# Order of the first loads in a fused attention and feed-forward kernel: a load ahead of the identity, beacon keys on another queue, up weights ahead of the masks

## The chip, the cores and the metric

The kernel runs on one core of a Trainium2 chip. The metric is device time in microseconds (us), the lower the better. A profiled execution has a span, from the first to the last instruction, and a time of its own, which is a little longer.

## The reference

Attention over 8 sequences of 8 heads, 576 tokens and 64 dimensions, with 16 "beacon" keys and values in front that every query sees; behind it a feed-forward layer without bias, with a leaky ReLU.

```python
k_all = np.concatenate([beacon_k, k], axis=2)
v_all = np.concatenate([beacon_v, v], axis=2)
scores = scale * np.matmul(q, k_all.transpose(0, 1, 3, 2))
causal[:, Nb:] = np.triu(np.ones((S, S), dtype=bool), k=1)
scores = np.where(causal, -1000000000.0, scores)
a = np.exp(scores - scores.max(-1, keepdims=True))
a /= a.sum(-1, keepdims=True) + 1e-09
x = np.matmul(a, v_all)          # then (batch, token, head*dim): 4608 x 512
h = x @ w_in                     # 512 x 2048
out = np.maximum(0.01 * h, h) @ w_out   # 2048 x 512
```

## The kernel before

The work is done by pairs of heads: pair `g` is heads 2h and 2h+1 of sequence `g // 4`, so there are 32 pairs, four to a sequence. Everything is in bf16 with sums in float32.

For a pair, `t_q` (L229, L235) turns queries and keys on TensorE (PE) with an identity matrix and copies them out of PSUM. `score` (L253, L262) makes the transposed scores in four parts on PE, and ScalarE (ACT) takes the exponential into `aT`. `mask` (L275) zeroes the upper triangles of `aT` on GpSimd (POOL), five selects for a pair. `value` (L342 to L352) multiplies by the values, with a column of ones that yields the sums, and VectorE (DVE) divides. `x_transposes` or `x_turn` put the result into `xT`. From then on `up` (L395, L402) makes one 128-wide block of the hidden layer for 512 tokens, and `down` (L433) a quarter of an output tile. PE alternates between these and the attention of later sequences; the last part is feed-forward alone. From pair 8 on queries and keys are loaded in natural order (`load_natural`, L157) and turned by DMA from SP (`turn_pair`, L165).

Each engine executes its instructions in the order in which the program text issues them. For the head, the first eight pairs, this order is written out by hand in strings of steps that `run` reads. `l3.0` loads pair 3's queries and `l3.1` its keys (L145), `V1.2` value block 2 of sequence 1 (L200), `s2.1` is part 1 of pair 2's scores, `m2.1` a part of its masks, `q3` and `k3` its transposes, `v0.0` the first half of pair 0's values, `x1` the transpose of its result, `u` and `d` an up and a down step, `i0` and `i1` the two halves of the up weights (L118), `o0` and `o1` of the down weights (L124), `N8.0` and `T8` pair 8's loads and turns. `w6` and `W0.0.4` are blank matmuls whose results nobody reads.

All loads that change the type from float32 to bf16 are issued by GpSimd, on one queue, between its masks. The beacon keys are loaded as float32 into `bk_raw` (L171): those of sequences 0 and 1 from ScalarE, those of sequences 2 to 7 in one load of 128 x 6 x 64 elements (192 KB) from SP. They are cast to bf16 into `bk`, the later ones by GpSimd (L174) after pair 6's masks; PE then turns them (L180) and they are copied to the key tiles of pairs 8 and on. The text has the load from SP after `s3.3`, but no earlier instruction stands in SP's list except the load of pair 0's keys `first_k` (L151), so SP issues it in the first microseconds.

In the built program GpSimd's loads take eight completion semaphores in turn, and a load waits on its semaphore for the load eight places ahead of it to land.

Of the kernel before, what the change touches and what calls it, by code (L numbers as in the profile page):

```python
# [15 lines left out]
def kernel(  # L16
# [11 lines left out]
    nc = tc.nc  # L28

    B, H, S, D = q.shape  # L30
# [112 lines left out]
    def load_qk(g, which):  # L143
        b, hp, grp, rows = where(g)
        loaded["qk", g, which] = nc.gpsimd.dma_start(  # L145
            out=raw_of(b, grp)[which][rows],
            in_=(q, k)[which][b, 2 * hp : 2 * hp + 2].rearrange("h (p i) d -> p h i d", i=RI),
        )
# [21 lines left out]
    def load_beacon_k(b0, b1, eng):  # L170
        eng.dma_start(out=bk_raw[:, b0:b1], in_=beacon_k[b0:b1].rearrange("b h n d -> (h n) b d"))  # L171
# [19 lines left out]
    def load_v_cast(b, c):  # L191
        dst = v_bufs[b % 2]
        lo = 0
        if c == 0:
            nc.gpsimd.dma_start(
                out=dst[0:NB, 0, :, 0:D], in_=beacon_v[b].rearrange("h p d -> p h d")
            )
            lo = NB
        n = ROWS[c] - lo
        nc.gpsimd.dma_start(  # L200
            out=dst[lo : ROWS[c], c, :, 0:D],
            in_=v[b, :, OFF[c] : OFF[c] + n].rearrange("h p d -> p h d"),
        )
# [9 lines left out]
    def beacon_columns(g, copy):  # L213
        b, hp = divmod(g, NPAIR)
        copy(out=k_bufs[g % NK][:, 0:NB], in_=bkT[:, b, hp])
# [26 lines left out]
    def score(g, n):  # L242
        qT, kT = qk[g]
        if n == 0:
            probs[g] = a_bufs[g % NA]
        aT = probs[g]
        parts = SCORES[n]
        sc = ps_sc.tile([128, 2, 512], FP32, name="sc", tag="sc")
        c0 = parts[0][3]
        for c, q0, w, col in parts:  # L250
            for par in range(2):
                ps_ = slice(par * 64, par * 64 + 64)
                nc.tensor.matmul(  # L253
                    out=sc[:, par, col - c0 : col - c0 + w],
                    lhsT=kT[ps_, c * 128 : (c + 1) * 128],
                    rhs=qT[ps_, q0 : q0 + w],
                    start=True,
                    stop=True,
                    skip_group_check=True,
                )  # L260
        w = sum(p[2] for p in parts)
        nc.scalar.activation(  # L262
            out=aT[:, :, c0 : c0 + w], in_=sc[:, :, 0:w], func=AF.Exp, scale=0.125
        )
# [3 lines left out]
    def mask(g, part):  # L268
        aT = probs[g]
        for lo, n, rows in MASKS[part]:  # L270
            triangle(aT, lo, n, rows)
# [231 lines left out]
    def finish(g, eng=0):  # L503
        if eng < 2 and g in xs:
            x_transposes(g, (dve, act)[eng])
        ready[0] = chunks_with(g)
        if g % NPAIR == NPAIR - 1:
            turn[0] = 1

    def run(steps):  # L510
        for step in steps.split():
            op, a = step[0], [int(x) for x in step[1:].split(".")] if step[1:] else []
            if op == "s":
                score(*a)
            elif op == "m":
                mask(*a)
            elif op == "v":
                value(*a)
            elif op == "x":
                finish(*a)  # L520
            elif op == "l":
                load_qk(*a)
            elif op == "V":
                load_v_cast(*a)
            elif op == "N":
                load_natural(*a)
            elif op == "T":
                turn_pair(a[0])
            elif op == "y":
                x_turn(a[0])  # L530
            elif op == "q" or op == "k":
                t_q(a[0], 0 if op == "q" else 1, (dve, act)[a[1] if len(a) > 1 else 0])
            elif op == "b":
                beacon_columns(a[0], (dve, act, pool)[a[1]])
            elif op == "u":
                up()
            elif op == "P":
                moe1_early(*a)
            elif op == "d":
                down()  # L540
            elif op == "w":
                unused(*a)
            elif op == "W":
                unused_ahead(*a)
            elif op == "i":
                load_w_in(a[0])
            elif op == "o":
                load_w_out(a[0])
            else:
                raise ValueError(step)  # L550
# [11 lines left out]
    with order:  # L562
        load_first_keys()
        load_beacon_k(0, 2, nc.scalar)
        nc.vector.memset(blank, 0.0)  # L565
        run("l0.0")
        make_identity(nc, ident)
        make_ones()
        run("l1.0 l1.1 l2.0 l2.1 V0.0 V0.1 V0.2 l3.0 l3.1 V0.3 V0.4 l4.0 l4.1")
        make_pads()  # L570
        unused(24)
        cast_beacon_k(0, 2, nc.scalar.copy)
        beacon_transposes(0, 2)
        unused(10)
        nc.scalar.copy(out=k_nat0[:, :, 0], in_=first_k[:, 0])
        nc.vector.tensor_copy(out=k_nat0[:, :, 1], in_=first_k[:, 1])
        run("q0.1 k0 w6 s0.0 m0.0 q1 s0.1 k1 w6 s0.2 m0.1 w6 s0.3 m0.2 i0")
        run("w6 s1.0 m1.0 q2 s1.1 k2 w6 s1.2 m1.1 w6 s1.3 m1.2 W0.0.4 s2.0 m2.0 W0.0.4 s2.1 q3 l5.0 l5.1 W0.0.4 s2.2 k3 v0.0 m2.1 s2.3 m2.2 i1 W0.1.4 s3.0 m3.0 v1.0 s3.1 v0.1 s3.2 v1.1 m3.1 l6.0 l6.1 s3.3 x0.1 m3.2")
        load_beacon_k(2, B, nc.sync)
        run("v2.0 l7.0 l7.1 q4 v2.1 V1.0 V1.1 x1 k4.1 v3.0 v3.1 x2.1 s4.0 s4.1 x3 m4.0 V1.2 V1.3 V1.4 u s4.2 u s4.3 m4.1 m4.2 o0 u q5 k5 u")  # L580
        run("s5.0 s5.1 m5.0 u u s5.2 s5.3 m5.1 m5.2 o1 u q6 k6 u v4.0 u v4.1 s6.0 s6.1 m6.0 u y4 N8.0 N8.1 u s6.2 s6.3 m6.1 m6.2 u")
        cast_beacon_k(2, B, nc.gpsimd.tensor_copy)
        run("q7 u k7 u v5.0 u v5.1 y5 N9.0 s7.0 s7.1 m7.0 d v6.0 v6.1 d y6 T8 s7.2 s7.3 m7.1 m7.2 N9.1 T9")
        beacon_transposes(2, B)
        run("b8.2 b9.2 b10.2 b11.2 u v7.0 v7.1 d d d d N10.0 N10.1 V2.0 V2.1 V2.2 V2.3 V2.4 d d N11.0 N11.1 x7")


        CUTS = [(0, 512, 1024, 1536, 1664), (0, 384, 896, 1376, 1664), (0, 224, 736, 1248, 1664)]
        BLOCKS = [((0, 0),), ((0, 1),)], [((0, 2),), ((0, 3), (1, 0))], [((1, 1),), ((1, 2),)], [((1, 3), (2, 0)), ((2, 1),)], [((2, 2),), ((2, 3),)]
        FIRST = 2 * NPAIR  # L590

        def block(g0, i):
            for tile in BLOCKS[i]:
                stretch([(g0 + r, CUTS[r][n], CUTS[r][n + 1]) for r, n in tile])

        events = []
        for g in range(FIRST, NG):
            if g > FIRST + 3:
                events.append((g - 3.6, 0, run, ("N%d.0" % g,)))
                events.append((g - 3.1, 0, run, ("N%d.1" % g,)))  # L600
            if g > FIRST + 1:
                events.append((g - 2.0, 0, run, ("T%d" % g,)))
            if g > FIRST + 3:
                events.append((g - 1.9, 0, run, ("b%d.2" % g,)))
            events.append((g + 2.25, 3, value, (g, 0)))
            events.append((g + 2.62, 4, value, (g, 1)))
            events.append((g + 2.63, 5, x_turn, (g,)))
            if (g - FIRST) % 3 == 0:
                for i in range(5):
                    events.append((g + (0.31 if g == FIRST else 0.01) + 0.6 * i, 2, block, (g, i)))  # L610
        ends = [FIRST]
        for g in range(FIRST, NG):
            events.append((g + 3.5, 2, finish, (g, 2)))
            if g % NPAIR == NPAIR - 1:
                ends.append(g + 3.5)
        for b in range(3, B):
            for n in range(NKB):
                events.append((4 * b - 0.9 + 0.3 * n, 6, load_v_cast, (b, n)))
        events.sort(key=lambda e: e[:2])
        KEPT = 3  # L620
        first_down[0] = 4
        w, d0 = 0, done1[0] + done2[0]
        for at, _, what, args in events:
            while w + 2 < len(ends) and at > ends[w + 1]:
                w, d0 = w + 1, done1[0] + done2[0]
            todo = 2 * NF * ready[0] - KEPT - d0
            aim = d0 + todo * (at - ends[w]) / (ends[w + 1] - ends[w])
            while done1[0] + done2[0] < aim and fill():
                pass
            what(*args)  # L630
        while done2[0] < NCH * NF:
            fill()
# [30 lines left out]
```

## Time and profile before

| What | Value |
|---|---|
| Median of 4 runs (lowest to highest) | 342.98 us (341.84 to 346.03) |
| Profiled execution: its own time, its span | 342.78 us, 341.1 us |
| Granted TensorE clock, mean | 0.997 |
| Busy: PE, ACT, POOL, DVE | 331.7, 186.8, 180.4, 81.8 us |
| First up matmul on PE | 25.26 us |
| Landing of the first load of queries | 5.47 us |
| Landing of the second half of the up weights | 31.15 us |

The profile lists busy time of each engine, the chain of waits that ended last, and groups of instructions by line of the program. In the timelines the columns are the start and the length in us, then engine, line, operation, the tile written and the tile read, and in brackets the idle time ahead and what ended it. A load has two times: the issue, for which the engine is busy, and the landing, given as a time after the start of the issue.

### The profile page before, as it was taken

The numbers are of one execution on the slowest core, as the hardware profiler recorded it, in microseconds if no ns is written. First come the engines' busy times: TensorE is split into PE (matmuls) and PEld (weight loads), VectorE is DVE, ScalarE is ACT, GpSimd is POOL, SyncE is SP. The second block draws the span as 40 slices with busy tenths as digits, with TensorE's granted clock in tenths as the row PEclk, the third lists the DMA queues.
The fourth block names the chain that finished last, engine by engine and source line by source line (L and its number), as shares of the span: only waits on it lengthen the run. The fifth ranks groups of instructions, "written<-read, shape, count | busy, mean of one in ns | idle before, by whom it ended". The sixth has DMA issues, their size and how long they took to land.

```text
span 341.1 us, 7423 instructions
## 1 busy us (share of the span) xinstructions
PE 331.7 (97%) x2982; PEld 167.7 (49%) x2982; DVE 81.8 (24%) x199; ACT 186.8 (55%) x280; POOL 180.4 (53%) x354
## 2 busy tenths in 40 slices
PE   8899899999998999999999999999999999999995
PEld 6573455445453545454454554544555544444442
DVE  4372344121232113221222122212321220000111
ACT  4978662669643864479257753775457205633300
POOL 8995768889997686398476854772211000000000
PEclk9999999999999999999999999999999999999998
DMA  8999999999999998999999999998220120000021
GB/s 156 149 211 174 129 185 153 184 156 165 167 145 177 168 134 109 152 124 144 122 146 120 118 151 122 158 122 79 81 82 17 32 97 33 0 31 33 31 92 62
DMA packets 155042, 40.16 MB, mean 118 GB/s; under 512 B 145152, under 2 KB 149376, under 8 KB 155008
## 3 DMA queue, kind: packets, MB, share of 16 engines
q0 software_dynamic: 100784, 18.34, 74.9%
q1 hardware_dynamic: 53808, 21.16, 33.0%
q8 instruction: 23, 0.38, 0.5%
q10 hardware_dynamic: 416, 0.20, 0.2%
q14 instruction: 11, 0.09, 0.1%
HBM read 37.22 MB, written 9.44 MB: 137 GB/s over the span
## 4 chain that ended last, share of the span: by engine, by line
PE 77%; DMA 13%; POOL 7%; SPq 1%; issue 1%; DVE 0%; ACT 0%; POOLq 0%
PE acc L395 33%; PE acc L433 30%; PE av L342 7%; PE sc L297 5%; DMA v_aug<-in_v_dram 4%; DMA w_in_sb<-in_moe_w_in_dram 4%; POOL aT L275 2%; DMA k_nat<-in_k_dram 2%; DMA xT<-x_nat 2%; POOL v_aug L200 2%; DMA q_raw<-in_q_dram 1%; PE sc L253 1%; POOL k_nat L157 1%; PE tp L229 1%; PE av L483 1%
## 5 line engine op out<-in xcount | busy, mean ns | idle before, releaser
L395 PE MATMUL acc<-xT,w_in_sb 128*128 128x512 bf16 x576 | 139.0, 379 | 1.4 <-DMA xT<-x_nat 1.4
L433 PE MATMUL acc<-w_out_sb,gT 128*128 128x512 bf16 x576 | 136.6, 379 | 0.0
L402 ACT ACTIVATE gT<-acc 128x512 bf16<-128x512 f32 x144 | 85.2, 606 | 80.0 <-PE acc L395 79.3
L310 ACT ACTIVATE aT<-sc 128x1024 bf16<-128x1024 f32 (+3 forms) x96 | 76.8, 866 | 47.4 <-PE sc L297 45.7
L275 POOL TENSOR_SCALAR_AFFINE_SELECT aT<-aT 128x256 bf16<-128x256 bf16 (+2 forms) x160 | 58.0, 396 | 67.6 <-ACT aT L310 61.0
L433 PEld LDWEIGHTS <-gT 128*128 128x128 bf16 x576 | 53.7, 98 | 62.3 <-issue 2.5
L395 PEld LDWEIGHTS <-w_in_sb 128*128 128x128 bf16 x576 | 52.2, 98 | 60.5 <-issue 2.7
L445 DVE COPY osb<-acc 128x512 f32<-128x512 f32 x35 | 24.2, 692 | 92.1 <-PE acc L433 91.4
L351 DVE RECIPROCAL rec<-av 128x6 f32<-128x6 f32 (+1 forms) x64 | 12.1, 188 | 135.5 <-PE av L342 135.5
L342 PEld LDWEIGHTS <-aT 128*128 128x128 bf16 (+1 forms) x960 | 36.3, 98 | 14.1 <-issue 4.2
L342 PE MATMUL av<-v_aug,aT 128*128 128x65 bf16 (+1 forms) x960 | 40.3, 194 | 0.9 <-POOL aT L275 0.7
L200 POOL DMA_DIRECT2D v_aug<-in_v_dram x40 | 34.1, 861 | 4.2 <-DMA w_in_sb<-in_moe_w_in_dram 4.0
L157 POOL DMA_DIRECT2D k_nat<-in_k_dram x48 | 34.8, 730 | 2.3 <-DMA v_aug<-in_v_dram 1.2
L157 POOL DMA_DIRECT2D q_nat<-in_q_dram x48 | 34.8, 729 | 2.3 <-DMA v_aug<-in_v_dram 1.4
L352 DVE TENSOR_TENSOR x_nat<-av,rec 128x384 bf16<-128x384 f32 (+1 forms) x64 | 31.4, 491 | 2.2
L262 ACT ACTIVATE aT<-sc 128x1024 bf16<-128x1024 f32 (+3 forms) x32 | 26.4, 877 | 4.4 <-PE sc L253 4.4
L297 PE MATMUL sc<-qT,kT 64*128 64x208 bf16 (+16 forms) x368 | 24.4, 255 | 0.2 <-POOL aT L275 0.2
L297 PEld LDWEIGHTS <-kT 64*128 64x128 bf16 x368 | 12.3, 94 | 19.2 <-issue 16.5
L253 PE MATMUL sc<-qT,kT 64*128 64x80 bf16 (+4 forms) x96 | 10.1, 285 | 0.3 <-DVE kT L235 0.3
L235 DVE COPY qT<-tp 128x576 bf16<-128x576 bf16 x7 | 5.3, 756 | 16.6 <-PE tp L229 13.2
L451 ACT COPY osb<-acc 128x256 f32<-128x256 f32 x1 | 0.4, 372 | 13.7 <-DVE osb L449 13.7
L483 PE MATMUL av<-blank 128*128 128x128 bf16 x70 | 6.8, 260 | 1.1 <-DVE blank L565 1.1
(43 smaller groups left out, 67.5 us busy)
## 6 DMA issues: line engine op xcount, KB each, us to landing
out_dram<-osb SPq DMA_DIRECT2D x35, 256.0 KB, 2.5
q_nat<-in_q_dram POOLq DMA_DIRECT2D x48, 72.0 KB, 4.4
k_nat<-in_k_dram POOLq DMA_DIRECT2D x48, 72.0 KB, 4.4
v_aug<-in_v_dram POOLq DMA_DIRECT2D x24, 128.0 KB, 6.0
w_in_sb<-in_moe_w_in_dram POOLq DMA_DIRECT2D x2, 1024.0 KB, 11.3
w_out_sb<-in_moe_w_out_dram POOLq DMA_DIRECT2D x2, 1024.0 KB, 11.8
q_raw<-in_q_dram POOLq DMA_DIRECT2D x8, 144.0 KB, 7.5
k_raw<-in_k_dram POOLq DMA_DIRECT2D x7, 144.0 KB, 8.1
```

The costliest lines, as they stand in the source:

```text
L157: nc.gpsimd.dma_start(out=t[:, :, par], in_=(q, k)[which][b, 2 * hp + par].rearrange("(t p) d -> p t d", p=NR),)
L200: nc.gpsimd.dma_start(out=dst[lo : ROWS[c], c, :, 0:D], in_=v[b, :, OFF[c] : OFF[c] + n].rearrange("h p d -> p h d"),)
L262: nc.scalar.activation(out=aT[:, :, c0 : c0 + w], in_=sc[:, :, 0:w], func=AF.Exp, scale=0.125)
L275: nc.gpsimd.affine_select(out=view, in_=view, compare_op=ALU.is_ge, fill=0.0, base=128 - n if lo == 0 else 0, channel_multiplier=-1, patte ...
L297: nc.tensor.matmul(out=sc[:, par, at : at + b - a], lhsT=kT[ps_, c * 128 : (c + 1) * 128], rhs=qT[ps_, q0 : q0 + b - a], start=True, stop= ...
L310: nc.scalar.activation(out=probs[g][:, :, lo:hi], in_=sc[:, :, at : at + hi - lo], func=AF.Exp, scale=0.125)
L342: nc.tensor.matmul(out=avv[:, n, 0 : D + 1], lhsT=aT[0 : ROWS[c], par, a0 : a0 + 128], rhs=va[0 : ROWS[c], c, 2 * hp + par, :], start=(c = ...
L352: nc.vector.tensor_tensor(out=x_nat[:, t0:t1].rearrange("p t e d -> p (t e) d"), in0=avv[:, :, 0:D], in1=rec[:, n0:n1, None].to_broadcast( ...
L395: nc.tensor.matmul(out=acc, lhsT=w_in_sb[:, j, fc * 128 : (fc + 1) * 128], rhs=xT[:, j, i * 512 : (i + 1) * 512], start=(j == 0), stop=(j ...
L402: nc.scalar.activation(out=gT[i][:, fc, :], in_=acc, func=AF.Prelu, alpha=0.01)
L433: nc.tensor.matmul(out=acc, lhsT=gT[i][:, fc, t * 128 : (t + 1) * 128], rhs=w_out_sb[:, fc, :], start=(fc == 0), stop=(fc == NF - 1),)
L445: nc.vector.tensor_copy(out=osb, in_=acc)
```

## The change

Four edits in the part that is ordered by hand. `l1.0` (pair 1's queries) is issued ahead of the identity. `i0` goes from behind pair 0's masks to behind the last load of the first string, and so ahead of these masks on GpSimd's list. In the second string `v0.0` goes from behind `k3` to ahead of `q3`, four blank matmuls between `q3` and `s2.2` are dropped, and `i1` goes ahead of `m2.2`. The load of the later beacon keys goes from SP to GpSimd, behind `o0` and so between the two halves of the down weights.

```diff
         load_beacon_k(0, 2, nc.scalar)
         nc.vector.memset(blank, 0.0)
-        run("l0.0")
+        run("l0.0 l1.0")
         make_identity(nc, ident)
         make_ones()
-        run("l1.0 l1.1 l2.0 l2.1 V0.0 V0.1 V0.2 l3.0 l3.1 V0.3 V0.4 l4.0 l4.1")
+        run("l1.1 l2.0 l2.1 V0.0 V0.1 V0.2 l3.0 l3.1 V0.3 V0.4 l4.0 l4.1 i0")
...
-        run("q0.1 k0 w6 s0.0 m0.0 q1 s0.1 k1 w6 s0.2 m0.1 w6 s0.3 m0.2 i0")
-        run("w6 s1.0 m1.0 q2 s1.1 k2 w6 s1.2 m1.1 w6 s1.3 m1.2 W0.0.4 s2.0 m2.0 W0.0.4 s2.1 q3 l5.0 l5.1 W0.0.4 s2.2 k3 v0.0 m2.1 s2.3 m2.2 i1 W0.1.4 s3.0 m3.0 v1.0 s3.1 v0.1 s3.2 v1.1 m3.1 l6.0 l6.1 s3.3 x0.1 m3.2")
-        load_beacon_k(2, B, nc.sync)
+        run("q0.1 k0 w6 s0.0 m0.0 q1 s0.1 k1 w6 s0.2 m0.1 w6 s0.3 m0.2")
+        run("w6 s1.0 m1.0 q2 s1.1 k2 w6 s1.2 m1.1 w6 s1.3 m1.2 W0.0.4 s2.0 m2.0 W0.0.4 s2.1 v0.0 q3 l5.0 l5.1 s2.2 k3 m2.1 s2.3 i1 m2.2 W0.1.4 s3.0 m3.0 v1.0 s3.1 v0.1 s3.2 v1.1 m3.1 l6.0 l6.1 s3.3 x0.1 m3.2")
         run("v2.0 l7.0 l7.1 q4 v2.1 V1.0 V1.1 x1 k4.1 v3.0 v3.1 x2.1 s4.0 s4.1 x3 m4.0 V1.2 V1.3 V1.4 u s4.2 u s4.3 m4.1 m4.2 o0 u q5 k5 u")
+        load_beacon_k(2, B, nc.gpsimd)
         run("s5.0 s5.1 m5.0 u u s5.2 s5.3 m5.1 m5.2 o1 u q6 k6 u v4.0 u v4.1 s6.0 s6.1 m6.0 u y4 N8.0 N8.1 u s6.2 s6.3 m6.1 m6.2 u")
```

## The prediction

> **What bounds the kernel now.** I read the page's busy shares first, then the chain of waits, then the head in the timeline of each engine, and last the DMA view in short stretches.
>
> ```profile
> PE 331.7 (97%) x2982; PEld 167.7 (49%) x2982; DVE 81.8 (24%) x199; ACT 186.8 (55%) x280; POOL 180.4 (53%) x354
> ...
> PE 77%; DMA 13%; POOL 7%; SPq 1%; issue 1%; DVE 0%; ACT 0%; POOLq 0%
> ```
>
> PE is busy for 331.7 of 341.1 us. So an edit can gain only where PE still waits, and all the large waits lie before 40 us and at 107 us. The chain of waits leaves PE for DMA and POOL in 20% of the span. Its first half shows where:
>
> ```profile
> 12.12 1.73 POOL aT L275 x5
> 13.85 0.71 POOL w_in_sb L118
> 14.56 2.06 POOL aT L275 x6
> ...
> 19.06 12.10 DMA w_in_sb<-in_moe_w_in_dram
> 31.15 0.29 issue
> 31.44 0.89 POOL v_aug L200
> 32.55 6.05 DMA v_aug<-in_v_dram
> 38.60 0.04 issue
> 38.64 0.63 PE av L342 x15
> ```
>
> GpSimd works through a full list until 19 us. Then the second half of the up weights lands at 31.15 us, and only then does GpSimd issue the rest of sequence 1's values, for which PE waits. Why GpSimd waits there is in the built program: its loads take eight completion semaphores in turn, and each load waits for the load eight places ahead of it. The timeline of GpSimd shows that wait, and the two others that matter here:
>
> ```profile
> 12.02 1.83 POOL L275 TENSOR_SCALAR_AFFINE_SELECT aT<-aT 128x224 bf16<-128x224 bf16 x5
> 13.71 0.85 POOL L118 DMA_DIRECT2D w_in_sb<-in_moe_w_in_dram  x1
> ...
> 31.44 0.89 POOL L200 DMA_DIRECT2D v_aug<-in_v_dram  x1 [3.96 <-DMA w_in_sb<-in_moe_w_in_dram]
> ...
> 45.46 0.49 POOL L174 CAST bk<-bk_raw 128x384 bf16<-128x384 f32 x1
> 45.90 1.44 POOL L157 DMA_DIRECT2D q_nat<-in_q_dram  x2
> 49.04 0.38 POOL L275 TENSOR_SCALAR_AFFINE_SELECT aT<-aT 128x224 bf16<-128x224 bf16 x1 [1.70 <-ACT aT L262]
> ```
>
> PE's timeline shows what the head's loads cost: it stands until pair 3's queries land at 15.05 us, and ACT then idles 0.69 and 0.51 us between exponentials.
>
> ```profile
> 15.05 0.47 PE L229 MATMUL tp<-ident,q_raw 64*64 64x64 bf16 x18 [0.87 <-DMA q_raw<-in_q_dram]
> ```
>
> **1. The beacon load leaves the head.** It is 192 KB that SP issues at 1.61 us. By 5 us the first keys have landed (0.81 + 3.9), so what the hardware queue carries from 5 to 7 us is this load alone:
>
> ```profile
> q0 software_dynamic: 329, 0.34, 101.4%
> q1 hardware_dynamic: 380, 0.09, 23.4%
> ```
>
> The DMA engines are full then: the shares add to 125%, and loads behind land 7 to 9 us after issue against 4.1 for the first one. The load has 128 x 6 = 768 rows, so 380 packets are half of it. Their cost is 23.4% of 2 us = 0.47 us, or 0.38 us when scaled down to a sum of 100%. The other half goes before 5 us, where the same view shows gaps; it costs from nothing to another 0.48 us. So everything on GpSimd's queue behind it lands 0.4 to 0.95 us earlier. I take 0.6. The gain lasts, since the queue keeps a backlog: landings follow in the order of issue (first up half 24.2, second 31.15, pair 6's queries 32.2).
>
> The Trainium skill ("DMA: Bandwidth & Descriptors", section "Issuing engines are not separate DMA queues") says that DMAs started by any engine end on the same 16 DMA engines and interleave, so another issuer saves only sequencer time. That speaks against this part: by it alone the move from SP to GpSimd gains 0, and what I count comes from the move in time, which the 23.4% row supports.
>
> **2. The second query load ahead of the identity.** It is issued at about 2.07 instead of 2.60 us (the memset and the select stand at 2.06 and 2.37). The identity is then ready at 3.2 instead of 2.66 us. PE first needs it at 3.74, and the blank matmuls cover that; without them it would be free too, as bk is cast at 3.21. Pair 1's queries land some 0.5 us sooner, but ACT runs ten exponentials without a stop from 7.16 to 15.47 us. I cost both at nothing.
>
> **3. The first up weights ahead of the masks.** Same place among the loads, so the same load eight places ahead: the second value block of sequence 0. It is the second of three value loads that start at 5.48 and take 2.64 us, so it is issued at 6.36 us; it lands 6.9 us later (DMA view, issues from 6.0 to 6.4 us), at 13.26 us. Before, the five masks of pair 0 covered that wait. Now GpSimd stands from 12.06 until that landing, 13.26 - 0.6 = 12.66 us, issues for 0.85 us, and starts the masks at 13.5 instead of 12.02. Queued behind are all masks of pairs 0 to 3 and the loads of pairs 5 and 6. From pair 1's masks on only the idle 0.6 us remains as delay, since the issue itself was already in front of them. Pair 3's last mask ends at 23.2 + 0.6 - 0.2 (an idle gap at 20.8) = 23.6 us. PE used it for matmuls ending at 24.3, so this is late by nothing to 0.2 us. The second up half passes two masks (2 x 0.36 us) and pays 0.6: it is issued at about 19.0 as before, and lands by the queue, 0.6 earlier.
>
> **4. PE's order.** v0.0 (12 matmuls, 0.54 us) goes ahead of pair 3's transposes and four blank matmuls (0.37 us) go. v0.0 needs two mask parts: 13.5 + 3 x 0.36 = 14.6 us, and pair 3's queries now land at 14.45. It ends about 15.0, the transposes at 15.4, so that score 2.2 comes at 15.4 instead of 15.76 and score 2.3, no longer behind v0.0 and the blanks, at 16.1 to 16.4 instead of 17.18. ACT's idle 1.2 us shrinks to 0.4 or so. The first up matmul, now at 25.26, moves by -0.85 (both idles gone) to +0.2 us (no relief, masks held until 13.26): I take -0.5.
>
> **5. What decides at 38 us.** The value load at 31.44 waits for the up half. With that at 30.55 it is issued at 30.8, and PE's waits of 0.67 and 0.23 us end 0.6 earlier. PE arrives 0.5 earlier, so it still waits there. PE is at -0.6 us.
>
> **6. The beacon load in its new place.** Issued after the first down half (35.51 - 0.6 + 0.89), for about 0.86 us, the row of a value load with as many rows. Behind it stand pair 5's masks and the second down half. Pair 5's values come on PE at 45.6, 7 us later. On the queue it adds 0.4 to 0.95 us ahead of the second down half (51.5 us) and pair 8's loads (55.1); with the 0.6 gained they stay where they are. The third down step at 53.63 needs the former, with 2 us of room. The cast on GpSimd is the new wait. It is reached at 45.46 - 0.6; the load lands after the first down half (35.51 + 10.2 = 45.7, less 0.6, plus 0.6 to 0.95), at about 45.9. GpSimd stands 1 us; behind it are two query loads and pair 7's masks, which wait 1.70 us for ACT anyway. Cost nothing; with that cover gone, 1 us.
>
> **The sum.** -0.6 at 38 us. From 53 us on loads start when ACT releases GpSimd's masks, and land 4.1 to 4.4 us after issue, so they move with PE; the queue ahead of them does not, and I let 0.1 us be lost there and at 107 us, where PE waits 1.43 us for a transpose. -0.5 us against the profiled execution's own 342.78 (span 341.1) gives 342.3. The median of the runs shown is 342.98, 0.2 above it, and they spread from 341.84 to 346.03; about 1%, 3.4 us, is what a measurement of this kernel can tell from no change.
>
> **Rivals.**
> The gain is absorbed: the queue is full from 38 us on with the beacon rows added back, and PE waits at 72.9 and 107 us take it. For it: at 72.02 us the masks wait behind loads that wait for values. Against it: landings of 4.1 us at 55 us show no backlog there. 342.8.
> A larger gain: the relief is the full 0.95, both of ACT's idles go (1.2) and PE meets no wait at 37 to 39 us (0.9, if the value blocks come 1.5 early). Against it: these gains stand in one line, not side by side, so 0.95 + 0.9 is the bound: 340.9.
> Slower, by the beacon cast: the load lands with the second down half at 51.5 us instead of behind the first. It decides once the cast begins after 49.04 - 1.44 - 0.49 = 47.1 us. At 51.5 pair 7's first mask goes to 53.4, five masks of 0.37 end at 55.2 instead of 53.3, and the loads of pairs 9 and 10, PE's v7.0 and the beacon transposes come 1.9 late: 342.8 - 0.6 + 1.9 = 344.1, and up to 3 us more if the values of sequence 2, which land 8.5 us after issue, push the masks at 72 us out as well. For it: the new load has six rows of 256 bytes in each of 128 partitions, and the small-row value blocks took 2.9 us where larger rows took 1 (10.4 to 13.26). Against it: loads landed in order.
> The Trainium skill (same page, "Queues, rings and completion order") says that each DMA engine serves the queue rows in turn, packet by packet. By it a load on SP's own row would pass the down weights, while on GpSimd's it stands behind 1 MB; no row here shows the two beside each other.
>
> **How the numbers follow.** Forecast 0.47, absorbed 0.20, larger gain 0.12, slower by the cast 0.21. The forecast's own range is 341.7 to 343.0. The time is 342.3; the range goes down to 340.4 for most of the larger gain, and up to 345.9 for most of the cast's. Over 1% faster needs 339.5, below every case: 0.10 for what I have not seen and for spread. Over 1% slower needs 346.4, the cast's far end: 0.18. Within: 0.72.
>
> **What would show it.** Right: GpSimd idle 0.3 to 0.9 us before the first up weights near 12.1 us; v0.0 on PE before 15 us; the second up half landing at 30.2 to 30.8; the value load after it moved alike; an idle of about 1 us before the beacon cast and none after; PE's wait at 107 us within 0.3 of 1.43. Wrong: the second up half at 31 us or later, a cast later than 47 us, or PE waiting in 52 to 73 us where it now has no more than 0.24.

## The result, and the profile after

The changed kernel takes 345.65 us in the median, the kernel before 344.33 us on the same chips: a ratio of 1.0041, 95% interval 1.0026 to 1.0057. It is 1.4 us slower, where 0.5 us less was forecast. The profiled execution took 343.6 us (span 341.9) against 342.78 (341.1). Executions of one kernel spread over several microseconds (before: 341.84 to 351.49), so below a profile shows a mechanism and the ratios its price; they leave out the executions of any kernel that fell in a slower state.

The page of the kernel after, busy shares and chain:

```profile
PE 332.2 (97%) x2978; PEld 168.2 (49%) x2978; DVE 81.7 (24%) x199; ACT 186.9 (55%) x280; POOL 181.1 (53%) x355
...
PE 83%; DMA 10%; POOL 3%; SPq 1%; issue 1%; DVE 0%; ACT 0%; POOLq 0%
```

Less of the chain lies on DMA and POOL than before (13% for 20%), and still the span is longer. GpSimd's timeline:

```profile
12.81 0.78 POOL L118 DMA_DIRECT2D w_in_sb<-in_moe_w_in_dram  x1 [0.70 <-DMA v_aug<-in_v_dram]
13.59 3.75 POOL L275 TENSOR_SCALAR_AFFINE_SELECT aT<-aT 128x224 bf16<-128x224 bf16 x11
...
30.94 2.48 POOL L200 DMA_DIRECT2D v_aug<-in_v_dram  x3 [3.59 <-DMA w_in_sb<-in_moe_w_in_dram]
...
45.79 0.50 POOL L174 CAST bk<-bk_raw 128x384 bf16<-128x384 f32 x1 [0.86 <-DMA bk_raw<-in_beacon_k_dram]
...
48.21 0.38 POOL L275 TENSOR_SCALAR_AFFINE_SELECT aT<-aT 128x224 bf16<-128x224 bf16 x1 [0.54 <-ACT aT L262]
```

All of this was forecast: the 0.70 us ahead of the up weights, masks from 13.59, the value load after the up half 0.5 us earlier, 0.86 us ahead of the cast, and the wait for ACT behind it smaller (0.54 for 1.70). PE had gained by then: one of its value steps of 30 matmuls starts 0.83 us earlier (first before, then after):

```profile
48.85 1.08 PE L342 MATMUL av<-v_aug,aT 128*128 128x65 bf16 x30
```

```profile
48.02 1.08 PE L342 MATMUL av<-v_aug,aT 128*128 128x65 bf16 x30
```

In this profile the gain goes in one place, which PE's timeline and the chain name:

```profile
61.90 0.61 PE L297 MATMUL sc<-qT,kT 64*128 64x512 bf16 x6 [1.78 <-DMA kT<-k_nat]
...
107.65 0.39 PE L395 MATMUL acc<-xT,w_in_sb 128*128 128x512 bf16 x1 [1.28 <-DMA xT<-x_nat]
```

```profile
54.71 1.22 SPq L165
...
56.04 5.72 DMA kT<-k_nat
61.77 0.14 issue
61.90 0.61 PE sc L297 x6
```

PE waits 1.78 us for the turned keys of pair 8. Before, the same scores started without a wait, 0.4 us after the keys had landed (60.47):

```profile
60.89 0.61 PE L297 MATMUL sc<-qT,kT 64*128 64x512 bf16 x6
```

```profile
54.48 1.22 SPq L165 DMA_TRANSPOSE qT<-q_nat  x1
55.81 1.20 SPq L165 DMA_TRANSPOSE kT<-k_nat  x1
```

Now the second query load of pair 8 lands at 54.56 instead of 53.26, the turn is issued at 56.04 instead of 55.81, takes 5.72 us instead of 4.66, and the keys land at 61.77. PE was ready for them at 60.12, 0.77 us earlier than before, so that much of the wait is its lead given back and 1.0 us is lost besides. Of the 1.30 us by which the keys come later, 0.23 is the later issue and 1.06 the longer turn; what made the turn longer, no run here separates.

### The profile page after: what moved, and what is told of

Its sections match the earlier page's. It is cut to its first block, busy times and chain, and to the rows that moved or that the text cites. A ratio compares the mean times of both kernels' runs of the same rounds, so it can differ in the third digit from the quotient of the medians.

```text
span 341.9 us, 7415 instructions
## 1 busy us (share of the span) xinstructions
PE 332.2 (97%) x2978; PEld 168.2 (49%) x2978; DVE 81.7 (24%) x199; ACT 186.9 (55%) x280; POOL 181.1 (53%) x355
## 4 chain that ended last, share of the span: by engine, by line
PE 83%; DMA 10%; POOL 3%; SPq 1%; issue 1%; DVE 0%; ACT 0%; POOLq 0%
PE acc L395 35%; PE acc L433 34%; PE av L342 8%; PE sc L297 6%; DMA v_aug<-in_v_dram 3%; DMA w_in_sb<-in_moe_w_in_dram 3%; DMA xT<-x_nat 2%; DMA kT<-k_nat 2%; POOL aT L275 1%; SPq L165 1%; POOL q_raw L145 1%; PE sc L253 1%; POOL k_raw L145 1%; SPq L376 0%; PE tp L229 0%
## 5 line engine op out<-in xcount | busy, mean ns | idle before, releaser
L402 ACT ACTIVATE gT<-acc 128x512 bf16<-128x512 f32 x144 | 85.2, 606 | 79.9 <-PE acc L395 79.2
L351 DVE RECIPROCAL rec<-av 128x6 f32<-128x6 f32 (+1 forms) x64 | 12.1, 189 | 138.1 <-PE av L342 138.1
## 6 DMA issues: line engine op xcount, KB each, us to landing
w_in_sb<-in_moe_w_in_dram POOLq DMA_DIRECT2D x2, 1024.0 KB, 11.4
```

The costliest lines, as they stand in the source:

```text
L402: nc.scalar.activation(out=gT[i][:, fc, :], in_=acc, func=AF.Prelu, alpha=0.01)
```

## Which of the four edits costs it: the load in the head, or the load behind the down weights

The change is split in two. The first kernel keeps the new order and puts the beacon load back on SP; the second is the old order with only the beacon load moved.

```diff
 e1_bk_sp, against after
+        load_beacon_k(2, B, nc.sync)
         run("v2.0 l7.0 ...")
-        load_beacon_k(2, B, nc.gpsimd)
```

> The changed kernel with the beacon load put back on SP in the first microseconds; the other edits stay. Theory (the load on GpSimd's queue ahead of pair 8's loads costs the time, because pair 8's keys then land too late at 62 us): the second up half lands near 31.1 us again, PE starts the first up matmul at 25.0 to 25.5, pair 8's keys are turned by 60.6 us, PE's wait for them is under 0.5 us (1.8 in the changed kernel), and the kernel is like the one before: ratio 0.997 to 1.002. Rival 1 (the masks held behind the first up weights, and v0.0 early, cost the time): the ratio stays at 1.003 to 1.006. Rival 2 (loads that move up with PE crowd the turns): PE does not move up here, so as the theory.

```diff
 e2_only_bk, against before
-        load_beacon_k(2, B, nc.sync)
         run("v2.0 l7.0 ...")
+        load_beacon_k(2, B, nc.gpsimd)
```

> The kernel before with only the beacon load moved to GpSimd's queue behind the first down half. Theory: up weights land 0.4 to 0.6 us earlier, PE is 0.5 us or so ahead at 40 us, pair 8's keys land 0.8 to 1.5 us later than 60.5 us, PE waits 1 to 2 us for them: ratio 1.002 to 1.006. Rival 1 (masks and v0.0): this leaves them as they were, ratio 0.996 to 1.000, no wait at 62 us. Rival 2 (crowding by loads that move up with PE): also a wait at 62 us, since PE and the loads are ahead by 0.5.

Measured: e1_bk_sp 1.003 [1.000, 1.006], e2_only_bk 1.0063 [1.0024, 1.0102]. The moved load alone is slower: its interval lies above 1. But the mechanism that was expected of it is not in its profile. PE does not wait for pair 8's keys there (they land at 60.79 and are used at 61.48); it is 0.59 us behind before at 48 us, not ahead, and waits longer at 109 us (1.43 before). In its head GpSimd stands 0.40 us ahead of a value load at 10.67 us, which waits for pair 2's keys, and its masks start at 12.58 for 12.02:

```profile
109.10 0.39 PE L395 MATMUL acc<-xT,w_in_sb 128*128 128x512 bf16 x1 [2.06 <-DMA xT<-x_nat]
```

The order edits alone are not a gain, though e1_bk_sp's profile (span 340.8) is a microsecond ahead of before at 60 us. Nor is a cost of the order shown: e7_sp_warm and e16_sp_more_blanks below, with the same order, SP's load in the head and more blank matmuls, came to 0.9975 and 0.9986. In e1_bk_sp GpSimd does not stand ahead of the up weights, and the gain melts later on PE:

```profile
12.02 0.88 POOL L118 DMA_DIRECT2D w_in_sb<-in_moe_w_in_dram  x1
```

```profile
72.55 0.49 PE L297 MATMUL sc<-qT,kT 64*128 64x224 bf16 x6 [0.95 <-DMA kT<-k_nat]
...
106.62 0.39 PE L395 MATMUL acc<-xT,w_in_sb 128*128 128x512 bf16 x1 [0.85 <-DMA xT<-x_nat]
```

The relief that the move was to bring does not last. Pair 4's keys, the last load of the first string but for the up half, are issued at 11.4 us and land at 19.51 us before, 19.37 after, 19.45 with the new order and the load in the head. The second up half lands at 31.15 before, 30.65 after, and earliest of the three, at 30.34, in e1_bk_sp, which has both the load in the head and the order. In e2_only_bk, which differs from before by the move alone, pair 4's keys land at 20.41 and the second up half at 31.62, both later.

All profiles of the new order, those further down too, say the same. Pair 1's queries, an early load, do land sooner without SP's load: at 5.87 to 7.01 us in eight kernels, at 7.01 to 7.26 in the five that have a load on SP in the head. Pair 4's keys no longer do: 19.33 to 20.37 without, 19.30 to 19.45 with. Nor does the second up half: 30.32 to 31.43 without, 30.15 to 30.49 with.

Then one suspect at a time: a sixth of the late load, twice the late load, none at all (in e3_bk_sixth and e10_none the keys not loaded are zeros), and pair 8's query and key loads ahead of the second down half.

```diff
 e3_bk_sixth, against after
+        nc.vector.memset(bk_raw[:, 3:B], 0.0)
-        load_beacon_k(2, B, nc.gpsimd)
+        load_beacon_k(2, 3, nc.gpsimd)
 e8_bk_twice, against after
         load_beacon_k(2, B, nc.gpsimd)
+        nc.gpsimd.dma_start(out=bk_two[:, 2:B], in_=beacon_k[2:B].rearrange("b h n d -> (h n) b d"))
 e10_none, against after
+        nc.vector.memset(bk_raw[:, 2:B], 0.0)
-        load_beacon_k(2, B, nc.gpsimd)
 e4_n8_first, against after
-   ... m5.2 o1 u q6 ... y4 N8.0 N8.1 u s6.2 ...
+   ... m5.2 N8.0 N8.1 o1 u q6 ... y4 u s6.2 ...
```

> The changed kernel with a sixth of the beacon load: the keys of sequence 2 alone, the other five sequences' beacon keys are zeros set by DVE in the first 3 us. So the head is free of the load and the later place nearly so. Theory: the relief stays and pair 8's loads come as early as PE: PE is 0.7 us ahead at 52 us and meets no wait over 0.5 us at 61 us; ratio 0.996 to 0.999. Rival 2 (what delays the turns is GpSimd's other loads that come 0.8 us earlier beside them, not the beacon rows): PE still waits 1 us or more at 61 us, ratio 1.001 to 1.004. Rival 1: ratio 1.002 to 1.005 without a wait at 61.

> The changed kernel with the beacon load issued twice in its new place, the second into a tile that nobody reads (0.86 us of GpSimd and another 768 rows ahead of the second down half). If the rows in that place are what costs: pair 8's loads land another 0.5 to 1 us later, the second down half too, PE waits 2.3 to 3 us near 62 us, ratio 1.006 to 1.009. If the place costs by the cast that waits on GpSimd, or not at all: 1.003 to 1.005.

> The changed kernel with no load of the later beacon keys at all (they are zeros, set by DVE in the first 3 us): neither in the head nor behind the first down half. Head theory: 1.002 to 1.005 like the changed kernel, pair 4's keys at 19.7 to 20.4 us. Late theory: 0.998 to 1.001, like the changed kernel with the load on SP. Relief as predicted: 0.996 to 0.999.

> The changed kernel with pair 8's four loads issued ahead of the second down half instead of behind pair 6's first mask. Theory: they land some 5 us earlier (near 49 us instead of 53 to 55.5), the second down half 1.5 to 2 us later (51.4 to 53.2), in time for its first use near 52.9; SP can turn pair 8 as soon as it has turned the results of pair 6 (53.3 us), the keys land by 59.8 us, PE has no wait there and keeps its 0.7 us: ratio 0.996 to 0.999. Rival 2 (crowding): the turn is slow whatever the loads do, PE waits 0.5 us or more, ratio 1.000 to 1.004. A new wait of PE for the second down half at 53 us would add up to 1 us.

Measured: e3_bk_sixth 1.0044 [1.0009, 1.0079], e8_bk_twice 1.004 [1.0001, 1.0078], e10_none 1.0012 [0.9978, 1.0046], e4_n8_first 1.0059 [1.0019, 1.0098]. These don't line up with the bytes of the late load: a sixth of it costs as much as twice, as far as intervals of 0.4% either way can tell. That something beside the late load is lost when SP's load leaves the head would explain it, but e10_none, which has neither load, does not show it: 1.0012, with an interval that holds both 1 and the 1.0041 of after. e4_n8_first removes the wait of 1.78 us (pair 8's loads land at 48 to 50 us, and PE does not wait for its keys) and buys another one, as the second down half now lands at 55.14:

```profile
55.18 1.02 PE L433 MATMUL acc<-w_out_sb,gT 128*128 128x512 bf16 x3 [1.32 <-DMA w_out_sb<-in_moe_w_out_dram]
```

## The TensorE clock

Some executions have a lower mean clock, after more often than before. A theory was that PE idles more in the changed head, loses its clock there, and that blank matmuls would cure it.

```diff
 e5_after_warm (after), e7_sp_warm (e1_bk_sp): both edits; e6_before_warm (before): the first, and W0.0.14 ahead of q3
-        unused(10)
+        unused(14)
-   ... i1 m2.2 W0.1.4 s3.0 ...
+   ... i1 m2.2 W0.1.14 s3.0 ...
```

> The changed kernel with more blank matmuls where PE idles in the head: four more ahead of pair 0's queries (5 us), ten more ahead of pair 3's scores (16.5 us). Clock theory (part of the cost is that PE's granted clock falls back to half in the head more often: the mean clock is 0.993 or less in 15 of 51 executions of the changed kernel and in 4 of 35 of the one before): at most 2 of 12 executions at 0.993 or less, and the ratio falls from 1.004 to 1.001 to 1.003. Beacon theory alone (the load's new place is the whole cost): the ratio stays at 1.003 to 1.006, since these blanks touch no load.

> The kernel before with the same four more blank matmuls at 5 us, and ten more ahead of pair 3's queries, where it waits 0.87 us. Clock theory: it is seldom throttled in the head as it is, so ratio 0.997 to 1.000. Beacon theory alone: 0.999 to 1.002, the blanks cost nothing or a little.

> The changed kernel with the beacon load back on SP and with the same blanks as in the warm changed kernel. If the new order of up weights, masks and v0.0 gains some 0.5 us and only the beacon load and the clock cost: ratio 0.995 to 0.999, the first up matmul at 24.5 to 25 us. If the gain of the order is taken back by waits at 62, 72 or 107 us whatever is done in the head: 0.999 to 1.002.

Measured: e5_after_warm 0.9996 [0.9961, 1.0031], e6_before_warm 1.0007 [0.9967, 1.0046], e7_sp_warm 0.9975 [0.9944, 1.0005]. e5_after_warm is below both ranges that were expected of it, but 3 of its 12 executions still have a mean clock under 0.9935, so the blanks did not keep the clock; the theory in this form is not supported, and why this kernel stands below after is not known. The clock comes back below, at another place.

## Both places at once

Three kernels have a load in the head and one behind the down weights; the tile `bk_two` of the added load is read by nobody.

```diff
 e9_head_and_late, against after
         load_beacon_k(0, 2, nc.scalar)
+        nc.sync.dma_start(out=bk_two[:, 2:B], in_=beacon_k[2:B].rearrange("b h n d -> (h n) b d"))
 e12_head_rows, against after: as e9, but the 192 KB are one row of 1536 bytes in each partition
+        nc.sync.dma_start(out=bk_two[:, 2:B].rearrange("p b d -> p (b d)"), in_=w_in_r[:, 0, 0:384])
 e11_before_late, against before: SP's load stays, and behind o0
+        nc.gpsimd.dma_start(out=bk_two[:, 2:B], in_=beacon_k[2:B].rearrange("b h n d -> (h n) b d"))
```

> The changed kernel with a second beacon load that nobody reads, on SP in the first microseconds, where the kernel before had it; so the load stands in both places. Head theory (taking the load out of the head does not make GpSimd's loads land earlier but later: pair 4's keys land at 19.4 to 19.6 us in four kernels with it and at 19.4 to 20.4 in six without): pair 4's keys at 19.4 to 19.7 us again, ratio 1.000 to 1.002. Late theory (the rows ahead of pair 8's loads are the whole cost): 1.003 to 1.005 like the changed kernel. Relief as I predicted it (the rows in the head cost 0.6 us): 1.005 to 1.007, pair 4's keys past 20.3 us.

> The kernel before, its beacon load left on SP, with a second one that nobody reads on GpSimd behind the first down half. Head theory: 0.999 to 1.002. Late theory: 1.003 to 1.005, the keys of pair 8 turned at 61 us or later and PE waiting for them.

> As the first of these four, but the idle load on SP has the same 192 KB as one row of 1536 bytes in each of 128 partitions instead of six of 256. If any load beside GpSimd's first ones helps: pair 4's keys at 19.4 to 19.7 us, ratio 1.000 to 1.002. If it has to be many small rows, or nothing helps: as the changed kernel, 1.003 to 1.005, pair 4's keys at 19.7 to 20.4 us.

Measured: e9_head_and_late 0.9994 [0.9954, 1.0035], e11_before_late 1.000 [0.9966, 1.0034], e12_head_rows 1.0025 [0.9984, 1.0066]. No cost of a load in the head shows in these. The sharpest pair is e11_before_late and e2_only_bk: the old order with the late load, once with a load on SP in the head (1.000) and once without (1.0063). So the late load alone is hardly the whole cost, though the two intervals still overlap. e9_head_and_late issued the up half at 12.04 us with no idle, like e1_bk_sp. That is the pattern to explain: in the new order, with a load on SP in the head, the second value block of sequence 0 lands at 11.40 to 11.44 us; without it, at 12.1 to 13.0, and GpSimd stands 0.2 to 1.1 us, with all masks behind it.

## Why the value block is early or late: a packet of instructions

A block is landed when its sixteenth part has come. The records of the block's semaphore show that fifteen parts come together, between 10.4 and 11.4 us after (10.95 and 11.3 before), and one alone at 12.53 (13.18 before). At that time the DMA view has one packet of another queue. For 9.0 to 9.8 us, columns packets, MB and share of 16 engines, first after, then e1_bk_sp:

```profile
q0 software_dynamic: 844, 0.11, 227.9%
q8 instruction: 1, 0.02, 11.8%
```

```profile
q0 software_dynamic: 980, 0.12, 255.0%
```

It is 16,384 bytes of instructions. The profile before has 23 such packets for 2982 matmuls and as many weight loads, with 65 to 165 matmuls between one and the next. That PE's progress sets its time is an inference: at its start 114 to 143 matmuls had begun, so it comes at no fixed count. It starts at 9.28 us before, at 9.09 after and at 9.85 in e1_bk_sp, and takes 1.3 to 1.5 us on its engine. In the profiles of all kernels but the last two below the border is sharp. Where the packet starts at 9.72 us or earlier (eleven kernels), the second value block lands at 12.5 to 13.6 us, in ten of them with the last part 0.9 to 2.3 us behind the fifteenth. Where it starts at 9.83 or later (five), the last two parts land within 0.04 us of each other, and in four of the five the last part of the next block is 1.4 to 2.0 us late. It is late by 0.2 to 2.5 us in the eleven as well, so late single parts are not the second block's alone. PE comes later to the place of the packet in e1, e7, e9 and e12, where the first queries land at 5.65 to 6.07 us (5.20 after), and in e3, where its clock is at half until 13 us.

The last four kernels test this and its price.

```diff
 e13_i0_back, against after
-   ... V0.3 V0.4 l4.0 l4.1 i0
+   ... V0.3 V0.4 l4.0 l4.1
-   ... w6 s0.3 m0.2
+   ... w6 s0.3 m0.2 i0
 e14_l1_only, against before
-        run("l0.0")
+        run("l0.0 l1.0")
-        run("l1.0 l1.1 l2.0 ...")
+        run("l1.1 l2.0 ...")
```

> After, with the first half of the up weights put back behind pair 0's masks (i0 behind m0.2); the beacon keys stay late, the second query load and v0.0 stay as in after. GpSimd now has masks to do while the second value block of sequence 0 lands. Theory A (what the missing load in the head costs is GpSimd's wait of 0.4 to 1.2 us ahead of the masks): masks of pair 0 start at about 12.0 us again, no idle stands ahead of the up weights, the ratio to the kernel before is 0.999 to 1.002, nearer to 1 than the 1.0041 of after. Theory B (the late beacon load itself, or the wait for pair 8's keys, costs it): the ratio stays at 1.003 to 1.006 and PE still waits over 1 us for kT at 60 to 63 us. Theory C (the PE clock in the head): the ratio follows the share of executions below a mean clock of 0.993.

> Before, with only the second query load put ahead of the identity; the beacon load stays on SP in the head, i0 behind the masks. If the quicker landing of the second value block of sequence 0 (11.4 us in all four kernels that have both an SP load in the head and the new order, 12.1 to 13.2 elsewhere) comes from the load's place ahead of the identity, it lands near 11.4 here; if it comes from the up weights' place behind it, it lands at 12.9 to 13.2 as before. My prediction's step 2 expects no change of the time: ratio 0.998 to 1.002; the rival, that an earlier start of GpSimd's queue gains what it is moved by, 0.5 us: 0.9985.

Measured: e13_i0_back 1.0008 [0.9971, 1.0045], e14_l1_only 0.9965 [0.9931, 0.9999]. With masks to do, GpSimd does not stand; the value block lands late (13.08) and nobody notices. In e14_l1_only the packet starts at 9.64 and the block lands at 13.62, in spite of SP's load in the head and the query load's new place: neither speeds the block.

Next, half as many blank matmuls of twice the width in after, so that PE reaches a given place of its work with fewer instructions behind it; and the opposite with SP's load in the head.

```diff
 e15_wide_blanks, against after
-        for i in range(n):
-            nc.tensor.matmul(out=ps[:, 0:cols], lhsT=blank, rhs=blank[:, 0:cols], ...)
+        for i in range(n // 2):
+            nc.tensor.matmul(out=ps[:, 0:256], lhsT=blank[:, 0:128], rhs=blank, ...)
 e16_sp_more_blanks, against e1_bk_sp
-        unused(10)
+        unused(22)
```

> After, with the blank matmuls of the head half as many and twice as wide (256 columns for 128), so that PE has the same work in time but some 26 matmuls and 26 weight loads fewer behind it at 9 us. In all sixteen profiles so far one packet of 16,384 bytes of instructions runs on one DMA engine between 8.7 and 10.4 us. Where it starts at 9.72 us or before, fifteen of sixteen parts of the second value block of sequence 0 land together and the last 0.9 to 2.3 us behind them; from 9.83 us on all sixteen land together. Code theory (the packet is asked for when PE has come so far in its list, and the engine that carries it delivers its part of the block late): the packet starts at 10.0 us or later, the block lands at 11.3 to 11.6 us though SP has no load in the head, the first half of the up weights is issued at 12.0 without an idle ahead of it; if GpSimd's wait is what costs the time, the ratio falls from 1.004 to 0.999 to 1.002. Rival (SP's load itself speeds the block): packet or not, the block lands at 12.5 to 13.1 and GpSimd stands 0.4 to 1.2 us. If the block comes early and the ratio stays at 1.003 or more, the wait is not the cost.

> After, with the later beacon keys back on SP in the head (as in e1_bk_sp) and 22 blank matmuls for 10 ahead of pair 0's transposes, in a time in which PE waits for the first queries (0.89 us in e1_bk_sp, 12 blanks of 0.073 us). PE then has 12 matmuls and 12 weight loads more behind it at 9 us. Code theory: the packet of instructions starts 0.4 us or more earlier than the 9.85 of e1_bk_sp; at 9.7 or before it, the second value block of sequence 0 lands at 12.5 to 13.6, and GpSimd stands 0.4 to 1.5 us ahead of the up weights although SP's load is in the head. Rival (SP's load itself speeds the block): it lands at 11.4 as in e1, e7, e9 and e12, up weights at 12.02. Time: by the wait's price the ratio is 1.002 to 1.005, by the rival 0.998 to 1.003; the landing tells more here than the ratio.

e15_wide_blanks did what the code theory says of the landing. The packet starts at 10.44 us, the block lands at 11.12 without a load on SP, and GpSimd does not stand:

```profile
11.42 0.68 POOL L145 DMA_DIRECT2D k_raw<-in_k_dram  x1
12.01 0.87 POOL L118 DMA_DIRECT2D w_in_sb<-in_moe_w_in_dram  x1
12.79 1.55 POOL L275 TENSOR_SCALAR_AFFINE_SELECT aT<-aT 128x224 bf16<-128x224 bf16 x4
```

The ratio is 0.9998 [0.9965, 1.003]. e16_sp_more_blanks missed its aim: the 22 blanks ran over, pair 0's transposes started at 6.20 us, and the packet came later (10.19), not earlier. The block landed at 11.14, as the border says, but the two theories were not told apart; 0.9986 [0.9956, 1.0015]. So the border of the landing holds in all eighteen profiles, and one kernel without SP's load, e15_wide_blanks, crossed it as forecast; that the packet itself delays the part, and is not delayed by the same thing, is not shown, since the trace does not tell which of the sixteen engines a packet or a part used.

## What the late load does at 62 us

Ten kernels carry the whole load behind the first down half. In four of their profiles PE waits 1.8 to 2.1 us for pair 8's keys: after, and the following three, e11_before_late (the old order), e13_i0_back and e15_wide_blanks:

```profile
62.62 0.61 PE L297 MATMUL sc<-qT,kT 64*128 64x512 bf16 x6 [1.81 <-DMA kT<-k_nat]
```

```profile
62.90 0.61 PE L297 MATMUL sc<-qT,kT 64*128 64x512 bf16 x6 [2.10 <-DMA kT<-k_nat]
```

```profile
62.28 1.04 PE L297 MATMUL sc<-qT,kT 64*128 64x512 bf16 x6 [2.02 <-DMA kT<-k_nat]
```

In the seven without it (before, e1, e6, e7, e10, e14, e16) PE does not wait for these keys. Where the wait appears, pair 8's second query load lands at 54.6 to 55.8 us, in the seven at 52.4 to 54.1; the turn of the keys is issued at 56.0 to 57.3 (54.5 to 55.8) and takes 5.4 to 5.7 us (4.2 to 5.4). But e11_before_late, e13_i0_back and e15_wide_blanks have ratios of 1.000, 1.0008 and 0.9998: the wait in one profiled execution does not tell the price of the kernel. In the last two the wait has a second part. The table by stretches for e15_wide_blanks (busy time and count of each engine, then PEclk, the granted clock):

```profile
core 0: us, PE busy (x) PEld busy (x) DVE busy (x) ACT busy (x) POOL busy (x), PEclk, DMA share, GB/s
59.00:62.30 3.30, 1.28 (x8) 0.44 (x8) 0.36 (x1) 0.60 (x1) 3.30 (x5) 1.00 1.87 165
62.30:65.70 3.40, 3.40 (x12) 1.18 (x13) 0.00 (x0) 1.94 (x2) 3.40 (x7) 0.50 1.82 197
65.70:69.00 3.30, 3.25 (x24) 1.42 (x24) 0.00 (x0) 1.47 (x3) 1.78 (x4) 0.99 1.72 201
```

PE is busy for 1.28 of 3.3 us, and for the next 3.4 us it runs at half clock: 12 matmuls where the stretch behind has 24. That is 1.7 us more. In after's profile the clock stayed whole.

One half-clock stretch of 3.41 us in 342 takes 0.005 off the mean clock (0.5 x 3.41 / 342). A mean under 0.9965 stands in 25 of 48 executions of after and in 38 of 140 of before; in 68 of 144 of the ten with the late load and in 56 of 208 of the seven without. Where in the span these stretches lie is known for the profiled ones alone. As an estimate, 20 more in 100 executions with a stretch of 1.7 us make 0.3 us of the late load's cost.

Single ratios have intervals of 0.3% either way, so the prices come from all together. A least-squares sum over 430 executions of the kernels told of here, with one term for each session on a chip, gives 0.73 us for a late load (95%: 0.37 to 1.09), 0.60 us for each us that GpSimd stands ahead of the up half (-0.01 to 1.2), and -0.18 us for the new order (-0.55 to 0.19). For after that is 0.73 + 0.7 x 0.60 - 0.18 = 1.0 of the measured 1.4 us. It is a fit to the runs that suggested its terms, and its figures move by some 0.1 us with how the sessions are grouped. GpSimd's standing cannot be told from the mere absence of the load in the head: that term in its place is as good, 0.76 us, and the late load then falls to about 0.5 us (0.1 to 0.95). With both terms in the sum, standing is left with 0.25 us for each us (-0.45 to 0.96), so no price of it is shown.

## Why the prediction was wrong, by its steps

**Step 1, the relief, failed, in the sentence "The gain lasts, since the queue keeps a backlog".** It put 0.6 us on everything behind the load on GpSimd's queue. Pair 1's queries do land at 5.87 us (7.01 before, 7.12 with step 2's edit alone). But pair 4's keys land 0.14 us earlier after than before, and within 0.1 us of e1_bk_sp; with the move alone (e2_only_bk) they land 0.90 us later. In between some loads come earlier, the fourth value block at 17.06 for 18.17, but it does so in e1_bk_sp too (17.30). The step took a share of the DMA engines at 5 to 7 us for a delay that lasts to 20 us. The share itself was misread: at 9.0 to 9.8 us the same row reaches 228 and 255%, so packets' times overlap, and 23.4% of 2 us is not 0.47 us of the engines. The section of the Trainium skill that it set aside ("DMA: Bandwidth & Descriptors", "Issuing engines are not separate DMA queues") put the gain at 0, and the runs are nearer to that.

**Step 2** shows no cost. It may gain: e14_l1_only, which is this edit alone, stands at 0.9965 with an upper end of 0.9999. One interval of sixteen that so nearly touches 1 is no proof, and nothing in its profile explains it: pair 1's queries land at 7.12 us, not earlier than before (7.01).

**Step 3 held in the profile,** 0.70 us of standing, masks at 13.59 for 13.5, the second up half at 19.20 for 19.0. But its landing at 12.66 us was the old 13.26 less a relief that is not there: that 12.53 came is luck, for with SP's load in the head the block lands earlier still (11.40 in e1_bk_sp). What the step had not seen is that fifteen of the block's sixteen parts had landed by 11.36 and it waits for one, in a profile where an instruction packet stood in the queue at that time. The same holds for the "small-row value blocks" of the cast's rival: of their 2.9 us, 1.89 are one part (11.29 to 13.18).

**Steps 4 and 5 held in their numbers.** ACT's idle shrinks from 1.20 to 0.79 us (forecast 0.4), the first up matmul is at 24.99 (forecast -0.5, measured -0.27), the second up half lands at 30.65 (forecast 30.55), and PE is 0.83 us ahead at 48 us. But e1_bk_sp, with the beacon load back in the head, is ahead by 1.04 us, so this gain goes with the order and not with the move. Nor does 30.65 prove the relief: kernels of the old order with SP's load in the head land that half at 30.61 (e6_before_warm) to 31.15.

**Step 6 failed with it, and is where the profile loses the time.** "With the 0.6 gained they stay where they are" was said of pair 8's loads. There was no 0.6 to set against the added rows, and the second query load came 1.3 us later (the last of the four, 55.30 for 55.74, did not). The turn behind them had 0.4 us of room (landing 60.47, use at 60.89), which the step did not look up, and its own lead of 0.6 us on PE would have used that up: it priced the third down step's 2 us of room and the cast, and stopped at the loads. By the fit the late load makes 0.5 to 0.7 of the 1.4 us, not all of it. The cast itself was covered as said, so the rival that ended slower named the wrong wait. "PE waiting in 52 to 73 us where it now has no more than 0.24" was the sign of failure that the text asked for, and it came.

**The rival of the absorbed gain** is true for the order edits: e1_bk_sp returns its lead at 72.6 and later. In e1_bk_sp, e7_sp_warm and e16_sp_more_blanks ACT's step behind an up block (L402) starts 1.04, 0.78 and 0.85 us ahead of before at 71 us, and 0.25, 0.01 and 0.54 us behind it at 80. So without any wait at 62 us the forecast gain would not have reached the end.

What is open: 0.4 us of the 1.4; whether GpSimd's standing or something else in the head is the second term, as e2_only_bk is slower with neither that standing nor the wait at 62 us; why only four of ten profiles show that wait, and why three of these four kernels are no slower than before.

## What to carry to other kernels

Follow a load that is added to a queue to the last user of every load behind it, and through each turn or cast in between, and write its room beside it: here 0.4 us of room on pair 8's turned keys counted, not 2 us on the down weights. A gap that is filled early on is a gain only if the next tight landing moves with it; a load that lands sooner at 6 us says nothing of the loads at 20 us. And before an instruction that waits for a landing is put ahead of ready work, look what makes that landing late: with masks to do, GpSimd did not stand (e13_i0_back, 1.0008), though no price of the standing is proven here.

## What the runs showed of the hardware

Code loading shows among the DMA packets. One packet of 16,384 bytes of instructions took 1.2 to 1.7 us while the queue was full; where it started at 9.72 us or earlier, the last part of one block landed 0.9 to 2.3 us behind the other fifteen in ten of eleven kernels, and half as many blank matmuls went with a start 1.35 us later (9.09 to 10.44).

The granted clock changes in steps of 3.41 us: full clock for 334.51 us before and after is 98 of them, and the half-clock stretches in e15_wide_blanks (62.32 to 65.73) and e13_i0_back (64.10 to 67.51) are one each. The Trainium skill ("TensorE: Matmul & The Clock Gate", Part 1) gives a free-running window of 3413 ns, and these rows agree. The waits at 62 us of 1.78 (after) and 1.81 us (e11_before_late) did not cost a window, those of 2.02 and 2.10 us did. The length of the wait does not decide it, though: at 107 to 111 us one of 2.06 us cost none in e2_only_bk, while one of 1.82 in e12_head_rows and one of 2.06 in e8_bk_twice each had a half-clock stretch with them.
